# A linear-attention block and a gated feed-forward block on one core: another order of the first loads, of the first products and of the whole plan

## The chip, the cores and the metric

The kernel runs on one core of a Trainium2 chip. The core has five engines that work side by side, each through its own queue in order: TensorE (PE in the profile; its weight loads are the row PEld), VectorE (DVE), ScalarE (ACT), GpSimd (POOL), and SyncE (SP), which in this kernel only starts transfers. ACT starts transfers too, from its own queue. The metric is the device time of one execution in microseconds; lower is better. The kernel before takes 274.34 us (median of three runs, 274.33 to 274.36).

## The reference

One layer over 2048 rows of 640 numbers, in bf16: an attention with a feature map (32 heads of 20), then a feed-forward block with a product as its gate, each behind a layer norm and with a residual.

```python
qkv = layernorm(x) @ wqkv                    # 640 -> 3 * 640, 32 heads of 20
pq, pk = q @ w_phi, k @ w_phi                # per head, 20 x 20
phi_q = concat(softmax(pq), softmax(-pq))    # 40 features per head; phi_k the same from pk
kv  = sum over rows of phi_k^T v ;  z = sum over rows of phi_k
o   = (phi_q @ kv) / (phi_q @ z + 1e-6)
h   = x + o @ wo
out = h + ((n @ w_gate) * (n @ w_up)) @ w_down,   n = layernorm(h);  640 -> 1536 -> 640
```

## The kernel before, in words

The 2048 rows are 16 row tiles of 128. The program is a list of named operations (`G.op`), each with an engine, the buffers it reads and writes, and a key. The string `PLAN` gives each name its key, the engine where there is a choice (`alts`, picked by the second field) and the buffer slots (third field: the eight PSUM banks, `xn`, `ek`, `ph` and the rest). `arrange` sorts by key: so the order on every engine and every transfer queue is written out by hand in `PLAN`, and an instruction that waits holds back everything behind it on its engine. `emit` puts in the semaphore waits that the buffers ask for. The numbers in a name are row tile, part or feed-forward block; the steps that the text speaks of:

- **Loads** (`dma`, L283 to L285; issued from SP or ACT): `x0`, `x1` ... rows of x, one or two tiles each (160 KB a tile); `wk0` to `wk4` and `wv0` to `wv4` the K and V columns of `wqkv` in five row blocks (160 KB each); `w5` the small feature weights; `wqt` the Q columns, turned by a DMA transpose (L309, SP); `wu`, `wg`, `wd`, `wo` the other weights (320 to 480 KB a piece).
- **Warm-up** (`warm`, L366 to L372): ten products of zeros, 512 wide, into PSUM, which need only a cleared buffer.
- **Folding the feature weights into `wk`**: `Ph` (L380) spreads `w5` into block-diagonal pieces; `WT` (L392) turns a row block of `wk` by five 128-wide products with the identity, `WTe` (L251) copies the result out of PSUM; `F1` (L411) multiplies it with the pieces, `Fe1` (L251) copies the folded weights out. `F0`, `Fe0` do this for Q later.
- **First layer norm**: `L1s`, `L1a` statistics (DVE, L428, L431), `L1l`, `L1e` the logarithm and exponential for 1/sqrt (ACT, L436, L439) for the groups of tiles in `LNG`, `L1n` a small product (POOL, L443), `xn` the normalised tile (L451 on ACT, L453 on DVE). Then the tile is turned: for the tiles in `TPE` by five products with the identity (`xt` on PE, L462, and a copy `xte`), for the others by a DMA transpose from SP (`xt`, L471).
- **Projections** (`proj`, L482): `K`, `V`, `Q` of a tile are ten products each of 128 x 320; for tiles 0 and 1 (`TSPLIT`) `K`, `V` (and `Q`) are cut in five pairs, one for each row block of the weights, so that a pair can start when its block is folded.
- **K side**: `Kx` exponentials (ACT, L494), `Ks` sums (DVE, L498), `Kr`, `Ke` their inverse (ACT, L501, L503), `Kn` the scaling (POOL, L518, 1280 wide), `Ve` the copy of V (L251), `KV` (PE, L526) adds the tile's outer products in two PSUM banks. After all 16 tiles `KVe` (DVE, L533) takes them out.
- **Q side**: `Qx` exponentials (ACT, L553, L554), `Qs` sums (DVE, L557), `Qr`, `Qe` (ACT, L560, L567) with a difference `Qb` (POOL, L564) between them, `Qn` the scaling of one half (POOL, L571, 660 wide), `qT` a DMA transpose (SP, L576).
- **Attention out**: `N` (PE, L589), `dd`, `rd`, `o` the division (DVE, L600 to L606), `oT` a DMA transpose (SP), `O` (PE, L616), `h` (DVE, L620), second norm `L2s`, `L2a`, `L2v` (POOL, L630), `L2r`, `hc` the centred tile (L639), `hT` a DMA transpose (SP, L643).
- **Feed-forward** in five blocks of 256 or 512 rows (`FB`): `U` (PE, L658) 24 groups of five products a block, gate and up; `g` (ACT, L663), `u` (DVE, L666); `D` (PE, L677) per row tile, `y` (DVE, L689), `w` the store (SP, L691). The last tile is cut in three column parts (`LASTCUT`).

The stretch in which all Q, K and V products stand runs from about 11 to 76 us; the first `N`, `O` and `U` are mixed in from 76 us on.

Of the kernel before, what the change touches and what calls it, by code (L numbers as in the profile page):

```python
# [48 lines left out]
x0:0.7:1 w5:1.18:1 wk0:1.18 wv0:4.06 wk1:2.14 wv1:2.62 wk2:1.66:1 wv2:3.58:1 wk3:2.62:1 wv3:4.06 wk4:3.1 wv4:4.54:1 x1:0.7 x2:2.14:1 x3:1.66 x4:3.58:1  # L49
x6:3.1 x8:5.02:1 x10:5.02 x12:4.54:1 x14:21.015 wqt0:13.874 wqt1:9.289 wqt2:26.055 wqt3:6.94 wqt4:19.655 wo0:27.415 wo2:34.715 wd0:35.195 wd1:47.175  # L50
wd2:49.392 wd3:37.595 wg0:32.875 wu0:5.5 wg1:37.115 wu1:6.46 wg2:40.335 wu2:25.575 wg3:36.635 wu3:5.98 wg4:35.675 wu4:36.155 id0:0.9 gl0:1.2 eps:0.7
id1:1.45 gla0:2.07 glb0:2.51 gla4:2.29 glb4:4.51 gla1:2.73 glb1:3.17 gla2:3.39 glb2:4.73 gla3:1.85 glb3:2.95 va1:6.664 phz:3.61 ekz:6.364 rqz:6.064
Sz:7.734 mk0:6.164 mk1:7.484 mk2:7.934 zero:0.7 warm0:1.08 warm1:1.51 warm2:1.94 warm3:2.37 warm4:2.8 warm5:3.23 warm6:3.66 warm7:4.09 warm8:4.52::0
warm9:4.74 Ph0:4.95 Ph1:5.609 Ph2:5.743:1 WT0:4.96::1 WTe0:5.509 WT1:6.769::5 WTe1:7.329:1 WT2:5.836::0 WTe2:6.386 WT3:7.725::2 WTe3:8.85 WT4:8.886::0
WTe4:9.922 F1_0:6.342::6 Fe1_0:8.676:1 F1_1:8.162::4 Fe1_1:9.299 F1_2:7.219::0 Fe1_2:8.052:1 F1_3:9.509::6 Fe1_3:10.766 F1_4:10.953::0 Fe1_4:11.538:1
L1s0:3.993 L1a0:5.633 L1s1:4.813 L1a1:6.1 L1s2:7.03 L1a2:9.686 L1s3:6.21 L1a3:10.215 L1s4:11.145 L1a4:12.785 L1s5:11.965 L1a5:13.005 L1s6:13.115
L1a6:14.353 L1s7:10.325 L1a7:12.895 L1s8:20.053 L1a8:21.803 L1s9:20.983 L1a9:23.833 L1s10:14.463 L1a10:20.873 L1s11:15.283 L1a11:19.443 L1s12:28.423
L1a12:34.233 L1s13:25.363 L1a13:30.243 L1s14:26.183 L1a14:34.123 L1s15:31.773 L1a15:34.013 L1l0:6.132 L1e0:7.229 L1l1:7.009 L1e1:7.952 L1l2:10.546
L1e2:11.389 L1n2:11.899 L1n3:11.699 L1l4:14.835 L1e4:15.678 L1n4:16.588 L1n5:16.188 L1n6:16.388 L1n7:15.988 L1l8:24.376 L1e8:24.806 L1n8:28.209
L1n9:28.409 L1n10:25.45 L1n11:25.65 L1l12:34.675 L1e12:35.518 L1n12:35.895 L1n13:36.095 L1n14:38.854 L1n15:36.295 xn0:7.85::0 xt0:8.53::3 xte0:9.268:1  # L60
xn1:8.35::1 xt1:9.165::1 xte1:9.796:1 xn2:12.875:1:3 xt2:17.252::7 xte2:17.978 xn3:12.161:1:2 xt3:13.17::0 xte3:13.935:1 xn4:19.553::2 xt4:21.495
xn5:17.025:1:0 xt5:18.295 xn6:18.943::1 xt6:22.855 xn7:23.333::3 xt7:24.215 xn8:29.243::1 xt8:30.155 xn9:29.743::3 xt9:31.515 xn10:26.408:1:0
xt10:27.895 xn11:27.745:1:2 xt11:33.355 xn12:36.631:1:0 xt12:45.815 xn13:36.758::1 xt13:38.075 xn14:39.692::2 xt14:47.712 xn15:38.118:1:3 xt15:40.815
V0_0:14.536::0 V0_1:14.807 V0_2:15.079 V0_3:15.351 V0_4:15.622 Ve0:20.238::2 K0_0:9.866::2 K0_1:10.138 K0_2:10.681 K0_3:12.083 K0_4:12.898
# [12 lines left out]
KV12:73.164 V13:60.939::4 Ve13:63.15:1:5 K13:50.484::2 Kx13_0:52.165::1 Kx13_1:52.998 Ks13:53.92::0 Kr13:56.436 Ke13:57.479 Kn13:57.839 KV13:73.479
V14:67.73::2 Ve14:69.782:1:7 K14:65.014::4 Kx14_0:66.642::3 Kx14_1:67.529 Ks14:68.362::3 Kr14:70.209 Ke14:70.659 Kn14:71.163 KV14:73.795 V15:70.447::6
Ve15:72.075:1:6 K15:59.58::2 Kx15_0:61.84::2 Kx15_1:62.733 Ks15:63.901::2 Kr15:65.742 Ke15:66.192 Kn15:67.259 KV15:74.11 KVe0:74.956 KVe1:74.696
F0_0:35.421::6 Fe0_0:36.006:1 F0_1:36.682::4 Fe0_1:37.345 F0_2:35.736::2 Fe0_2:37.258:1 F0_3:33.432::2 Fe0_3:34.895 F0_4:38.356::4 Fe0_4:38.941:1  # L80
# [837 lines left out]
```

## Time and profile before

| | |
|---|---|
| median of three runs | 274.34 us |
| the profiled execution: its span, first to last instruction | 272.2 us |
| what lies around the span, to the median | 2.14 us |
| PE busy | 266.0 us (98%), 2103 products |
| DVE, ACT, POOL busy | 171.0, 116.6, 73.9 us |
| TensorE clock granted, all stretches | 1.00 |
| HBM read, written | 11.00 MB, 2.62 MB |

The profile is of one execution; its own time is the span and the 2.14 us around it. A row names the line of the kernel, the engine, the operation and what it writes and reads. A recorded product includes its way through the array, so a 320-wide one is shown as 299 ns although the next starts 136 ns later (30 of them take 4.08 us in the chain of waits): starts tell more than busy time. Recorded spans on DVE and ACT likewise reach about 0.1 us into the next instruction's.

### The profile page before, as it was taken

Reading aid. Unit: us, or ns where it says so; the run is one execution under the profiler, and the core shown is the slowest. Engines: PE = TensorE matmul, PEld = TensorE weight load, DVE = VectorE, ACT = ScalarE, POOL = GpSimd, SP = SyncE. Lnnn points to the kernel's source line nnn. Section 1 sums busy time; section 2 is a strip of 40 time slices with the busy share of each in tenths; the row PEclk is TensorE's granted clock in tenths of the full one; section 3 lists DMA queues with packets and bytes.
Section 4 is the critical chain, followed back from the end, with each engine's and each line's share of the span. In section 5 each row is a group of like instructions: output and inputs, shape, how many; then the busy total and the mean of one; then the engine's idle time right before and its main releaser. Section 6 shows DMA issues by size and latency. Waiting matters only on the chain.

```text
span 272.2 us, 5234 instructions
## 1 busy us (share of the span) xinstructions
PE 266.0 (98%) x2103; PEld 177.2 (65%) x2103; DVE 171.0 (63%) x315; ACT 116.6 (43%) x307; POOL 73.9 (27%) x107
## 2 busy tenths in 40 slices
PE   7899999999989999999999999999999999999996
PEld 2777787777776788775555877766444457544774
DVE  4999978788899999897186147843324022314423
ACT  2999998987766746012213332300332220023000
POOL 7227996899974133200000000000000000000000
DMA  7997999987548998964022001531100001100011
GB/s 201 375 265 162 176 264 313 234 157 108 107 78 160 147 185 110 165 130 98 0 48 48 2 1 43 100 95 43 31 0 2 0 0 51 48 0 0 26 48 55
DMA packets 66600, 27.76 MB, mean 102 GB/s; under 512 B 57744, under 2 KB 65296, under 8 KB 66576
## 3 DMA queue, kind: packets, MB, share of 16 engines
q1 hardware_dynamic: 64752, 25.30, 45.2%
q10 hardware_dynamic: 1824, 2.13, 2.3%
q8 instruction: 16, 0.26, 0.5%
q14 instruction: 8, 0.07, 0.1%
HBM read 11.00 MB, written 2.62 MB: 50 GB/s over the span
## 4 chain that ended last, share of the span: by engine, by line
PE 93%; ACT 3%; DMA 2%; ACTq 1%; issue 0%; DVE 0%; DVEq 0%
PE ps L658 38%; PE ps L482 23%; PE ps L677 19%; PE ps L616 8%; DMA ev<-in_A_wqkv_dram 2%; PE ps L526 2%; ACT ph L553 2%; PE ps L589 1%; PE ps L411 1%; ACTq L285 1%; PE ps L462 0%; ACT ph L554 0%; PE ps L392 0%; ACT L884 0%; DVE Wp L689 0%
## 5 line engine op out<-in xcount | busy, mean ns | idle before, releaser
L658 PE MATMUL ps<-xnT,Wgu 128*128 128x512 bf16 (+1 forms) x600 | 105.2, 336 | 0.0
L658 PEld LDWEIGHTS ps<-xnT,Wgu 128*128 128x128 bf16 x600 | 58.5, 98 | 44.2 <-DVE ev L666 0.4
L663 ACT ACTIVATE gt<-ps 128x512 bf16<-128x512 f32 (+1 forms) x60 | 30.5, 511 | 91.4 <-PE ps L658 74.0
L482 PE MATMUL ps<-Wp,xnT 128*128 128x320 bf16 (+1 forms) x480 | 68.6, 299 | 0.8 <-ACT ph L554 0.8
L666 DVE TENSOR_TENSOR ev<-ps,gt 128x512 bf16<-128x512 f32 (+1 forms) x60 | 32.8, 577 | 47.4 <-PE ps L658 34.0
L482 PEld LDWEIGHTS ps<-Wp,xnT 128*128 128x128 bf16 x480 | 45.6, 97 | 18.4 <-ACT ph L554 0.9
L677 PE MATMUL ps<-Wd,ev 128*128 128x320 bf16 (+2 forms) x396 | 53.7, 295 | 0.0
L677 PEld LDWEIGHTS ps<-Wd,ev 128*128 128x128 bf16 x396 | 38.0, 98 | 14.5
L518 POOL TENSOR_TENSOR ek<-ek,SR 128x1280 bf16<-128x1280 bf16 x16 | 37.6, 2357 | 6.7 <-ACT SR L503 6.6
L689 DVE SCALAR_TENSOR_TENSOR Wp<-ps,rs,x_all 128x640 bf16<-128x640 f32 (+3 forms) x18 | 14.5, 808 | 32.9 <-PE ps L677 32.7
L553 ACT ACTIVATE ph<-ps 128x300 bf16<-128x300 f32 x64 | 23.8, 442 | 7.9 <-PE ps L482 7.4
L630 POOL TENSOR_SCALAR ln<-mv 128x1 f32<-128x1 f32 x16 | 3.3, 210 | 84.6 <-DVE mv L629 73.4
L557 DVE TENSOR_REDUCE S<-ph 128x66 f32<-128x1320 bf16 x16 | 24.2, 1515 | 3.1 <-ACT ph L554 3.1
L498 DVE TENSOR_REDUCE SR<-ek 128x64 f32<-128x1280 bf16 x16 | 23.4, 1472 | 1.3 <-ACT ek L494 1.2
L616 PE MATMUL ps<-Wo,Wp 128*128 128x320 bf16 x160 | 23.9, 299 | 0.3 <-ACT RQ L567 0.3
L494 ACT ACTIVATE ek<-ps 128x640 bf16<-128x640 f32 x32 | 22.3, 714 | 2.7 <-PE ps L482 2.4
L571 POOL TENSOR_TENSOR ph<-ph,RQ 128x660 bf16<-128x660 bf16 x16 | 20.9, 1307 | 6.2 <-ACT RQ L567 6.2
L639 ACT ACTIVATE xn<-x_all,mv 128x640 bf16<-128x640 bf16 x13 | 10.7, 828 | 24.2 <-DVE mv L629 24.2
L616 PEld LDWEIGHTS ps<-Wo,Wp 128*128 128x128 bf16 x160 | 15.2, 98 | 6.6 <-issue 0.6
L620 DVE TENSOR_TENSOR x_all<-ps,x_all 128x640 bf16<-128x640 f32 x16 | 13.0, 813 | 4.5 <-PE ps L616 4.4
L606 DVE TENSOR_TENSOR o<-ps,sm 128x720 bf16<-128x720 f32 x16 | 14.2, 894 | 0.1
L428 DVE BATCH_NORM_STATS2 st<-x_all 128x6 f32<-128x320 bf16 x16 | 7.6, 472 | 3.3 <-DMA x_all<-in_A_x_dram 3.3
(63 smaller groups left out, 171.4 us busy)
## 6 DMA issues: line engine op xcount, KB each, us to landing
out_dram<-Wp SPq DMA_DIRECT2D x15, 160.0 KB, 1.8
Wgu<-in_B_w_up_dram SPq DMA_DIRECT2D x5, 384.0 KB, 9.7
Wgu<-in_B_w_gate_dram SPq DMA_DIRECT2D x5, 384.0 KB, 7.0
Wd<-in_B_w_down_dram SPq DMA_DIRECT2D x4, 480.0 KB, 6.3
x_all<-in_A_x_dram SPq DMA_DIRECT2D x3, 320.0 KB, 6.8
x_all<-in_A_x_dram ACTq DMA_DIRECT2D x3, 320.0 KB, 9.1
Wp<-in_A_wqkv_dram SPq DMA_DIRECT2D x4, 160.0 KB, 7.4
x_all<-in_A_x_dram ACTq DMA_DIRECT2D x3, 160.0 KB, 4.9
```

The costliest lines, as they stand in the source:

```text
L482: ins = e.matmul(pb(b, hb)[:, 0:n1 - n0], lhsT=T["xnT"][:, NC - 1 - c, P * t:P * (t + 1)], rhs=T["Wp"][:, POS[kind], c, n0:n1], start=(c = ...
L494: G.op("act", "%sx%d_%d" % (nm, t, s), lambda e, s=s, b=b, ek=ek: e.activation(out=T["ek"][:, ek.slots[0], 0:2 * D].rearrange("p (b h s f) ...
L498: G.op("dve", "%ss%d" % (nm, t), lambda e, ek=ek, sr=sr: e.tensor_reduce(out=T["SR"][:, sr.slots[0], 0, :], in_=T["ek"][:, ek.slots[0], 0: ...
L518: G.op("pool", "Kn%d" % t, lambda e, ek=ek, sr=sr: e.tensor_tensor(out=T["ek"][:, ek.slots[0], 0:2 * D].rearrange("p (h f) -> p h f", f=DH ...
L553: e.activation(out=o_, in_=i_.rearrange("p (g j f) -> p g j f", j=3, f=DH), func=AF.Exp, scale=1.0 - 2.0 * sg)
L557: G.op("dve", "Qs%d" % t, lambda e, t=t, ph=ph: e.tensor_reduce(out=T["S"][:, t, 0:66].rearrange("p (g k) -> p g k", k=6), in_=pv(ph).rear ...
L571: return e.tensor_tensor(out=v, in0=v, in1=T["RQ"][:, rq.slots[0], 1, 0:33].rearrange("p (g j) -> p g j", j=3).unsqueeze(3).to_broadcast([ ...
L616: ins = e.matmul(pb(b, hb)[:, 0:320], lhsT=T["oT"][:, oT.slots[0], c, :], rhs=T["Wo"][:, c, 320 * hb:320 * (hb + 1)], start=(c == 0), stop ...
L658: ins = e.matmul(pb(b)[:, 0:n], lhsT=T["Wgu"][:, gu, c, P * ft:P * (ft + 1)], rhs=T["xnT"][:, NC - 1 - c, o0:o0 + n], start=(c == 0), stop ...
L663: G.op("act", "g%d_%d" % (bi, ft), lambda e, pg=pg, gt=gt, n=n: e.activation(out=T["gt"][:, gt.slots[0], 0:n], in_=pb(pg)[:, 0:n], func=AF ...
L666: o_ = G.op("dve", "u%d_%d" % (bi, ft), lambda e, pu=pu, gt=gt, hh=hh, ft=ft, n=n: e.tensor_tensor(out=T["hh"][:, hh.slots[0], ft, 0:n], i ...
L677: ins = e.matmul(pb(b, hb)[:, 0:w], lhsT=T["hh"][:, hh.slots[0], ft, P * tt:P * (tt + 1)], rhs=T["Wd"][:, ft, c0 + w * hb:c0 + w * (hb + 1 ...
```

## The change

It changes constants, gives four POOL operations a second engine, and replaces `PLAN`.

- `TPE` is (0, 1) where it was (0, 1, 2, 3): tiles 2 and 3 are turned by a DMA transpose from SP, which takes two times five products off PE, and two copies out of PSUM (`xte2`, `xte3`) off ACT and DVE.
- `NWARM` is 8 where it was 10; behind them come `NFILL` = 5 products of zeros, 256 wide, which stand between the first `WT` and `F1` in the new order.
- `LNG` groups the first layer norm finer: nine groups where there were six.
- `LASTCUT` cuts the last tile at 320 and 576 where it was 320 and 512.
- `L1n`, `Kn`, `Qb`, `Qn` and `L2v` may stand on DVE. In the new `PLAN` DVE has six `L1n`, six `Qb` (tiles 1, 2, 9, 10, 12, 14), four `Qn` (tiles 0, 1, 2, 4) and five `L2v`; no `Kn`. In turn two `Ve` are on DVE where it had six.
- `PLAN` has a new key for every operation. First loads: before, SP issued x1, w5, wk2, wk1, wv1, x6, wv2, wv3, wv4, x10, wu0, wu3, wu1, then three `wqt`; ACT issued x0, wk0, x3, x2, wk3, wk4, x4, wv0, x12, x8. After, ACT issues w5 and wk2 alone; SP issues x0, x1, wk1, wk0, x3, wk4, wk3, wv2, wv1, x4, wv0, x2, x6, wv3, wv4, then wqt1, xt3, x8, xt5, xt2, xt4. The large weights wu0, wu1, wu3 stand far later on SP, wu2 on ACT.
- PE's first products after: warm0 to warm7, WT2, warm8 to warm11, WT1, WT0, warm12, xt0, F1_2, F1_1, WT3, F1_0, WT4, xt1, F1_3, F1_4, then K0, K1, V1, V0 in pairs, V3, K3, V5, K2. Before, F1_4 and xt3 stood between those pairs, and xt2 behind V3.
- ACT after: L1l0, L1e0, WTe2, L1l1, L1e1, WTe0, xte0, Fe1_1, WTe3, Fe1_0, L1l3, L1e3, Fe1_3, xn3, Fe1_4.
- Around the first attention tiles PE has after: KV15, Q7, N0, N1, Q11, N2, Q8, N3, N9, Q14, O0, O1, O2, N4, O3, O9, Q12, N5, Q15, N7, then the first `U`. Before: KV15, Q7, N1, N3, N0, Q11, Q8, N2, Q14, N9, O1, O0, Q12, N5, O3, Q15, N4, N7, O2, O9, then the first `U`. In the new plan Q11 has the two PSUM banks that the KV sums leave; in the old one it had those of Q7.

```diff
-LNG = [[0], [1], [2, 3], [4, 5, 6, 7], [8, 9, 10, 11], [12, 13, 14, 15]]
-TPE = (0, 1, 2, 3)
+LNG = [[0], [1], [2], [3], [4, 5], [6, 7], [8, 9], [10, 11], [12, 13, 14, 15]]
+TPE = (0, 1)
-NWARM = 10
-LASTCUT = [(0, 320), (320, 512), (512, 640)]
+NWARM = 8
+NFILL = 5
+LASTCUT = [(0, 320), (320, 576), (576, 640)]
...
+    for k in range(NWARM, NWARM + NFILL):
+        G.op("pe", "warm%d" % k, lambda e: e.matmul(pb(wm_b)[:, 0:256], lhsT=T["zero"][:, 0:P], rhs=T["zero"][:, 0:256],
+             start=True, stop=True), 0.22, LT, [z_b], [wm_b], -89, before=[G.by["warm%d" % j] for j in range(k)])
...
-                G.op("pool", "L1n%d" % t, lambda e, t=t: e.tensor_scalar(
+                G.op("pool", "L1n%d" % t, lambda e, eng, t=t: e.tensor_scalar(
...
-                    op1=ALU.mult), 0.2, LP, [rs_b[t], mv_b[t]], [nb_b[t]], 10 * t - 25)
+                    op1=ALU.mult), 0.2, LP, [rs_b[t], mv_b[t]], [nb_b[t]], 10 * t - 25, alts=[("dve", 0.07, LD)])
...
-        G.op("pool", "Qb%d" % t, qb, 0.24, LP, [rq], [rq], kk)
+        G.op("pool", "Qb%d" % t, qb, 0.24, LP, [rq], [rq], kk, alts=[("dve", 0.1, LD)])
...
-        G.op("pool", "Qn%d" % t, qn, pool_c(660), LP, [ph, rq], [ph], kk)
+        G.op("pool", "Qn%d" % t, qn, pool_c(660), LP, [ph, rq], [ph], kk, alts=[("dve", dve_c(660), LD)])
...
```

More of the change, by code (lines that the diff above doesn't have):

```diff
@@ L48 @@
 for _t in """
[L49 to L64, printed above, removed]
@@ L77 @@
[L77 to L80, printed above, removed]
@@ new lines @@
+L1s1:4.207 L1a1:5.117 L1l1:6.053 wk1:1.74 L1e1:6.379 warm8:5.266::1 warm9:5.481 wk0:2.22:1 warm10:5.696 warm11:5.91 x3:2.7:1 xn0:5.226::0 gla4:3.14 WT1:6.125::2
+WTe1:6.745 glb4:3.369 WT0:6.543::3 wk4:3.18:1 gla3:3.509 glb3:3.737 Ph2:3.966 wk3:3.66 xn1:7.153::1 warm12:6.96 wv2:4.14:1 WTe0:7.162 Ph0:4.56 wv1:4.62
+L1s3:7.665 xt0:7.175::1 xte0:7.747 x4:5.1 gla2:5.154 glb2:5.383 Ph1:5.612 F1_2:7.454::4 Fe1_2:8.452 F1_1:7.772::6 Fe1_1:8.331 WT3:8.091::0 WTe3:8.915:1
+F1_0:8.508::2 Fe1_0:9.5:1 L1a3:9.192 WT4:8.828::1 WTe4:9.447:1 L1l3:10.084 L1e3:10.41 xt1:9.245::6 xte1:9.855:1 F1_3:9.676::4 F1_4:9.995::0 Fe1_3:10.503
@@ new lines @@
+L1s4:10.263 wv0:5.58:1 K0_0:10.314::2 K1_0:10.585::6 K1_1:10.856 K1_2:11.127 L1s5:11.05 L1n3:10.69 xn3:11.087:1:2 va1:10.914 Fe1_4:11.892:1 L1a4:11.837
+Sz:11.744 L1a5:11.96 L1l4:12.476 L1e4:12.802 x2:6.06 x6:6.54 L1s2:12.069 L1a2:12.979 L1l2:13.212 wv3:7.02 L1s7:13.088 wv4:7.5:1 L1e2:13.538 K0_1:11.398
+wqt1:7.98 xt3:12.03 K1_3:11.669 V1_0:11.94::4 K0_2:12.211 K0_3:12.482 K0_4:12.753 x8:13.34 L1n5:13.082 xn5:13.875::3 Kx0_0:13.631::0 Kx0_1:14.215 L1a7:14.387
+K1_4:13.024 xt5:14.5 Kx1_0:14.799::1 Kx1_1:15.383 V0_0:13.295::0 L1n4:13.306 V1_1:13.566 V1_2:13.837 V1_3:14.108 V1_4:14.379 xn4:15.967:1:0 L1n2:14.496:1
@@ new lines @@
+xn2:14.65::1 xt2:15.81 Ks0:15.162::0 Kr0:16.772 Ke0:17.063 Kn0:17.397 V0_1:14.65 V0_2:14.921 xt4:17.12 V0_3:15.192 V0_4:15.463 V3:15.734::2 Ve3:17.29::0
+L1s6:16.555 L1a6:17.465 Ve1:17.874::1 Ve0:18.458::2 Ks1:17.574::1 Kr1:19.086 L1l6:19.232 L1e6:19.558 Ke1:19.651 L1s9:18.967 L1a9:19.877 K3:17.09::6 L1n7:19.838
+xn7:20.14::2 L1s8:20.652 L1a8:21.562 V5:18.446::2 Ve5:20.002::3 K2:19.802::4 Kx3_0:20.586::2 Kx3_1:21.17 KV0:21.158::0,1 Kn1:20.062 L1l8:21.795 L1e8:22.121
+Kx2_0:22.214::3 K4:21.491::2 Ks3:21.906::2 L1n6:23.299:1 V2:22.847::6 L1n9:22.401 xn9:23.344::3 KV1:24.203 xn6:23.856::1 wqt3:18.43 Kx2_1:22.798 Ks2:24.368::3
```

184 lines of the change are left out of this document (93 added, 91 removed).

## The prediction

> **What bounds the kernel now.** I read the page's busy table first, then the chain of waits, then the timeline of the first 26 us and of the 76 to 96 us stretch, then the busy time by stretches.
>
> ```profile
> PE 266.0 (98%) x2103; PEld 177.2 (65%) x2103; DVE 171.0 (63%) x315; ACT 116.6 (43%) x307; POOL 73.9 (27%) x107
> ```
>
> PE is the bound. The chain says how much of its time is work:
>
> ```profile
> 3.25 6.60 DMA ev<-in_A_wqkv_dram
> 9.89 0.45 PE ps L392 x5
> ...
> 10.94 1.09 PE ps L482 x8
> ...
> 18.61 4.08 PE ps L482 x30
> ...
> 77.64 0.73 ACT ph L553 x2
> ...
> 252.37 17.30 PE ps L677 x132
> ...
> 269.76 0.42 DVE Wp L689
> ```
>
> A 320-wide product costs 0.136 us (4.08/30), so a ten-product K, V or O is 1.36, a Q 1.37, a KV or N 0.33, a turn by five 128-wide products 0.28 and an F1 0.32. Two places are not work. The chain begins with the load wk4, and the first projection starts at 10.78 (timeline); before it PE did seven turns and four F1, 7 x 0.28 + 4 x 0.32 = 3.24, so 7.5 us went to waiting and warm-up. The second: from Q7 (76.01) to the first U (95.74) PE does 6 Q, 8 N and 5 O, 6 x 1.37 + 8 x 0.33 + 5 x 1.36 = 17.7 of 19.7 us: 2.0 lost, the chain passing through ACT's exponentials. Elsewhere PE starts follow each other almost without a gap: about 0.4 us are lost between 11 and 76, none I can find after 96. So 9.9 us can be won at most by order, and the rest only by taking products away.
>
> ```profile
> 6.25 0.45 PE L392 MATMUL ps<-ident,ev 128*128 128x128 bf16 x5 [0.41 <-DMA ev<-in_A_wqkv_dram]
> 6.60 0.49 DVE L428 BATCH_NORM_STATS2 st<-x_all 128x6 f32<-128x320 bf16 x1 [0.41 <-DMA x_all<-in_A_x_dram]
> 7.25 0.69 ACT L251 ACTIVATE scratch<-ps 128x640 bf16<-128x640 bf16 x1
> 8.79 1.90 ACT L251 ACTIVATE Wp<-ps 128x640 bf16<-128x640 f32 x3
> 9.89 0.45 PE L392 MATMUL ps<-ident,ev 128*128 128x128 bf16 x5 [0.17 <-DMA ev<-in_A_wqkv_dram]
> ```
>
> These show arrival order: the fourth and fifth 160 KB load (wk2, x3) release work at 6.25 and 6.60, wk4, the tenth, only at 9.89. They also give the spacing on ACT: three copies of 640 in 1.90, 0.58 from start to start plus 0.7 for the last.
>
> **The change, part by part.** The profiled execution is 272.2 us of span; the median of the runs is 274.34, 2.14 more, and I carry that 2.14 over.
>
> *First loads and the fold.* In the new order wk0 is the fifth 160 KB load (x0, wk2, x1, wk1, wk0) and nothing of wv, x2 or the big weights stands ahead of the wk's. I let it land at 6.5, as the fifth did. Its turn starts 6.55, five starts 0.055 apart and 0.3 to the copy give WTe0 on ACT at 7.1. From there ACT is the chain: WTe0, xte0, Fe1_1, WTe3, then Fe1_0: 4 x 0.58 + 0.70 after 7.1 is 10.1, and the first K starts at 10.2. ACT is free to do this since it issues two loads where it issued ten (the last ended at 6.42, and WTe0 started at 6.46 although WT0 was done at 5.84). The other loads come in time: wk4 and wk3 are seventh and eighth, where the seventh (x2) released DVE at 7.78 and the ninth (wk3) PE at 8.67; the last wv has as many bytes ahead of it as before, where V1's pairs met no DMA wait from 13.3 on, and is asked for at 14. The next edge is Fe1_4: ACT does L1l3, L1e3 (0.4), Fe1_3, xn3 (0.81), Fe1_4 and ends at 12.6; PE asks for it nine pairs (9 x 0.272) after 10.2, at 12.65.
>
> Worth: the first K 0.55 earlier, with F1_4 (0.32) already behind it, and xt2, xt3 (0.56) not on PE at all: 1.4 us. Bounds: if loads land as the first four (by 4.6, then 0.45 each) the chain starts at L1e1, 6.6, and K at 9.7: 1.95. If one queue delivers slower, wk0 as late as the sixth load (wk1, used at 7.58), K starts at 11.25: 0.4. Fifteen loads at 0.4 to 0.6 of SP time each end at 8 to 9, which is before they land, so I stay with 1.4.
>
> *Tiles 2 and 3 by DMA.* xn3 ends at 11.9, SP's transpose takes 1.23 and lands 2.7 us after its start in the median, 9.9 behind six large weights (xt13). V3 asks for it 20 pairs after 10.2, at 15.7; the transpose lands at 14.6 to 15. Before it on SP stands wqt1, and such a transpose held SP 2.6 and 4.3 us at this time: from 8.0 to 10.6 or 12.3, the last a wait of 0.4 that still lands by 15.4. Cost 0, up to 1. xt5, xt2, xt4 follow with 1.3 us each for a tile that costs PE 2.72.
>
> *Warm-up and fills.* 8 x 0.43 end at 4.65, when wk2 is about there; the five fills stand where PE waits for wk1 and wk0. No cost.
>
> *Scaling on VectorE.* Not in the trace: a 660-wide scaling on DVE. Ends: 0.50, like the 640-wide xn (L453), and 1.31, like POOL's own. Nearest is o (L606, 720 wide, 0.894, next start at 0.81): I take 0.85. Four of these, six Qb at 0.1 to 0.24 and the L1n and L2v at 0.1 add 4.5 us to DVE; four `Ve` at 0.73 leave it. In the crowded stretch, from V9 to Q7 in the new order, PE has 17 projections and 7 KV, 25.5 us; DVE has 5 K sums (1.40), 8 Q sums (1.44), 4 Qn, 2 Ve and small ones, 23.6.
>
> ```profile
> 40.00:60.00 20.00, 20.00 (x193) 14.77 (x190) 16.96 (x14) 17.41 (x60) 16.14 (x11) 1.00 1.04 244
> 60.00:80.00 20.00, 19.20 (x210) 14.43 (x208) 17.61 (x21) 15.20 (x60) 18.09 (x18) 1.00 0.55 94
> 80.00:95.00 15.00, 14.66 (x148) 10.57 (x147) 14.79 (x28) 10.35 (x39) 5.19 (x9) 1.00 0.94 161
> ```
>
> (Columns: stretch, length, then busy PE, PEld, DVE, ACT, POOL, the granted clock, DMA share, GB/s.) So DVE keeps 1.9 us to spare: cost 0, but little cover. POOL loses 5 us of work it has room for.
>
> *The passage to attention out.* Q11 no longer waits for Q7's exponentials (the 0.96 us gap at 78.4) since it has the KV banks, and N, Q and O alternate. What remains is DVE: a tile's division is 0.11 + 0.28 + 0.81 = 1.2; three of them and the 0.5 of N come to 4.1 to 4.7 after N0, and PE asks for the third tile's banks (Q14) 5 x 0.33 + 2 x 1.37 = 4.4 after it. I leave 0.4 of the 2.0 lost: 1.6 won. Bounds: 2.0, and 0 if the waits only move. Transposes there land 2.6 (oT, hT) to 3.8 (qT) after issue, and one in the old run took 5.3; that is most of the 0.4.
>
> *Middle and end.* The 0.4 of small gaps stays. The last part is 256 wide, not 192: y at 0.42 gains 64 columns at 1.03 ns (0.88 at 640): 0.07 more. Feed-forward: same products, same copies, no gap before: 0.
>
> Sum: 272.2 - 1.4 - 1.6 + 0.1 = 269.3 of span, 271.4 us.
>
> **The rivals.**
>
> *VectorE and GpSimd block each other.* Place: 51 to 70 us, three Qb and four Qn on DVE while POOL is busy 80 to 90% with 2.36 us Kn and 1.31 us Qn. If a two-input DVE instruction waits for POOL's running one, five separate waits of half a Kn (1.18) are 5.9 us; 1.9 are spare, 4.0 reach PE through Qs, Qr and the Q banks: 275.4, slower. It decides from 4.9 us of waits (1.9 + 3.0); at 0.9 each it is a draw, 274.1. For it and against it:
>
> ```profile
> 4.70 1.07 POOL L380 TENSOR_TENSOR Phi<-w,GL 128x280 bf16<-128x280 bf16 x2 [1.00 <-DMA w<-in_A_w_phi_dram]
> 5.51 0.56 DVE L380 TENSOR_TENSOR Phi<-w,GL 128x280 bf16<-128x280 bf16 x1
> ```
>
> The one such DVE instruction, started while POOL did the same, took 0.56 where 280 columns at 1.03 to 1.13 ns and 0.13 fixed make 0.43: 0.13 too long, while POOL had 0.2 left. But xn on DVE is 0.59 with POOL idle (8.59) and 0.56 inside a Kn (20.12). [...] I give it 0.29: 0.17 for the draw, 0.12 for slower.
>
> *The passage gains nothing.* The exponentials of ACT, the oT transposes or DVE (99% busy from 80 to 95) make other gaps of the same 2.0: 273.0. For it: DVE's share. Against: DVE's rows there hold norm statistics that can wait. 0.10.
>
> *The clock or a load comes late.* The first eight wide products start 0.43 apart, later ones 0.22; the full rate is there at 5.39, after 4.1 us without a pause. New is a break at 4.65. If the rate came a few us later, 3.5 us of turns and F1 would take up to twice as long beside ACT's chain, or V3 waits 1 us for xt3: 272.6. 0.08.
>
> **How the numbers follow.** The forecast, 270.4 to 272.3, has 0.53: its low end is both gains at their bounds (0.5 + 0.4 below 271.4). The rivals hold 0.29, 0.10 and 0.08. Less than 0.2% (0.55 us) either way I call the same: 273.8 to 274.9. Faster is the forecast, the second and third rival, and a sixth of the draws: 0.74; same the rest of the draws, 0.14; slower 0.12. The range runs from 270.4 to 274.6: above lie the slower cases and few draws.
>
> **What would show it.** First K at 10.2 (not 10.8) in the timeline; V3 with no DMA wait; the L571 group on DVE near 0.85 us and POOL's Kn still 2.36 (right), or L571 and L564 on DVE at 1.5 and more with PE waiting for ACT ph between 60 and 76 (first rival); the PE share from KV15 to the first U at 17.7 of about 18.1 us; the last product ending near 266.8. I would be wrong if DVE, with 1.9 us spare in 25, is the bound of the whole projection stretch.

## The result and the profile after

The changed kernel takes 277.28 us (median of four runs, 277.18 to 277.77) beside 274.33 for the kernel before: ratio 1.0118, 95% interval 1.0104 to 1.0133. It is slower by 1.2%, where 271.4 was forecast. The profiled execution has a span of 275.4 us against 272.2, with the clock at 1.00 throughout.

The busy row of the page of after:

```profile
PE 266.6 (97%) x2096; PEld 176.6 (64%) x2096; DVE 180.3 (65%) x335; ACT 114.9 (42%) x311; POOL 67.7 (25%) x87
```

PE is still the bound, and DVE is busy 9.3 us longer than before: 3.9 of it are waits (below), and 3.0 are the `xn` of five more tiles, all done by 50.2 us, which the list of changes leaves out. The chain that ended last in after, in order of time (start, length, what), says where PE was not the last to be waited for:

```profile
10.32 9.52 PE ps L479 x70
...
35.14 6.79 DMA xnT<-xn
...
57.56 0.85 DVE RQ L561
58.41 1.51 DVE ph L568 x2
...
65.58 1.45 DVE RQ L561
...
68.47 2.38 DVE ph L568
70.85 0.75 DVE ev L247
...
90.96 5.24 DMA scratch<-ph
...
115.42 4.81 DMA Wp<-o
...
272.86 0.48 DVE Wp L687
```

The first K starts at 10.16 instead of 10.78 (timelines; the chain counts from the end of the product before, so it has 10.32), as forecast. Then come things that the chain of before did not have: a DMA transpose that took 6.8 us (xt11), a whole stretch of DVE in which `Qb` (L561, RQ) and `Qn` (L568, ph) last 0.85, 1.45 and 2.38 us, and two more transposes of 5.2 and 4.8 us (qT7, oT10).

I measured what PE lost from the starts of its products, less the time per product that the prediction gives:

| PE loses, us | before | after |
|---|---|---|
| until the first K | 7.5 | 6.6 |
| K6, F0_3, K11, K12: tiles and `wqt` that land late | 0.2 | 2.4 |
| V14, V13: PSUM banks that come free late (Qx13 on ACT behind `Qb2`, Ve12 on DVE behind `Qn2`) | 0 | 1.9 |
| from KV15 to the first U | 1.9 | 1.2 |
| O10: oT10 lands late | 0 | 0.9 |
| gaps below 0.15 | 0.4 | 0.7 |
| sum | 10.0 | 13.7 |

The sum is 3.7 more; the turns of tiles 2 and 3 that are no longer on PE take 0.56 off, and 3.1 of the 3.2 us of span are accounted for. The second row, in the timeline of after (start, length, engine, line; in brackets the idle time ahead and what ended it):

```profile
30.23 1.53 PE L479 MATMUL ps<-Wp,xnT 128*128 128x320 bf16 x10 [0.21 <-DMA xnT<-xn]
32.92 0.49 PE L408 MATMUL ps<-Phi,scratch 128*128 128x140 bf16 x6 [1.16 <-DMA scratch<-in_A_wqkv_dram]
```

K6 waits for xt6 and F0_3 for wqt0. xt6 was issued at 24.81 and landed at 30.18, wqt0 at 27.43 and 32.88: 5.4 us each, where a transpose with little ahead of it took 2.6 to 2.7 (xt4, xt9; 3.0 for wqt3). In SP's queue the new plan has x10, wg1, x12, wu4 and x14 in the 5.4 us ahead of xt6 (0.3 to 0.4 MB each), and wu1, wu3, wd2, wd1 right ahead of xt11, which took 6.8.

The third row, in the timeline of after, with a DVE instruction of another kind for comparison:

```profile
46.25 2.35 POOL L515 TENSOR_TENSOR ek<-ek,SR 128x1280 bf16<-128x1280 bf16 x1
47.60 0.60 DVE L450 TENSOR_SCALAR xn<-x_all,mv,rs 128x640 bf16<-128x640 bf16 x1
...
64.62 2.36 POOL L515 TENSOR_TENSOR ek<-ek,SR 128x1280 bf16<-128x1280 bf16 x1
65.50 1.52 DVE L561 TENSOR_TENSOR RQ<-RQ 128x32 f32<-128x32 f32 x1
67.79 2.35 POOL L515 TENSOR_TENSOR ek<-ek,SR 128x1280 bf16<-128x1280 bf16 x1
68.39 2.46 DVE L568 TENSOR_TENSOR ph<-ph,RQ 128x660 bf16<-128x660 bf16 x1
69.11 1.53 PE L479 MATMUL ps<-Wp,xnT 128*128 128x320 bf16 x10 [0.53 <-ACT ph L551]
71.64 0.44 PE L479 MATMUL ps<-Wp,xnT 128*128 128x320 bf16 x2 [1.00 <-DVE ev L247]
```

`Qb2`, 32 numbers wide, takes 1.52 us and ends at 67.03, 0.05 after POOL's Kn13 (66.98). `Qn2` takes 2.46 and ends 0.7 after Kn12 (70.15). Later `Qb`, with POOL idle, take 0.18, and the `Qn` that met nothing 0.83. So four of the ten waited: Qb1 0.2, Qb9 0.75, Qb2 1.35, Qn2 1.6, together 3.9 us. xn12, inside Kn8, did not wait. Nothing in the program makes `Qb2` wait for POOL; its one semaphore wait is for ACT. Behind `Qb2` on ACT's side stands Qe2 and behind that Qx13, for which V14 waits; behind `Qn2` on DVE stands Ve12, for which V13 waits.

The busy time by stretches in after (stretch, length, then PE, PEld, DVE, ACT, POOL):

```profile
40.00:60.00 20.00, 19.62 (x190) 14.25 (x189) 18.04 (x20) 18.32 (x64) 12.64 (x12) 1.00 0.84 158
60.00:80.00 20.00, 18.47 (x185) 13.17 (x184) 19.45 (x16) 15.31 (x55) 17.02 (x14) 1.00 0.91 212
80.00:95.00 15.00, 14.85 (x158) 10.82 (x157) 14.05 (x30) 8.85 (x32) 4.50 (x6) 1.00 0.91 144
```

DVE is at 19.45 of 20 us from 60 to 80, where it had 17.61, and PE falls from 19.20 to 18.47.

### The profile page after: what moved, and what is told of

Read it like the earlier page. It is cut to its first block, busy times and chain, and to the rows that moved or that the text cites. A ratio compares the mean times of both kernels' runs of the same rounds, so it can differ in the third digit from the quotient of the medians.

```text
span 275.4 us, 5224 instructions
## 1 busy us (share of the span) xinstructions
PE 266.6 (97%) x2096; PEld 176.6 (64%) x2096; DVE 180.3 (65%) x335; ACT 114.9 (42%) x311; POOL 67.7 (25%) x87
## 4 chain that ended last, share of the span: by engine, by line
PE 69%; DVE 18%; DMA 6%; ACT 3%; issue 1%; SPq 1%; DVEq 0%
PE ps L656 37%; PE ps L675 18%; PE ps L479 7%; PE ps L613 5%; DVE SR L495 4%; DVE S L554 4%; DMA xnT<-xn 2%; DMA scratch<-ph 2%; DMA Wp<-o 2%; DVE o L603 2%; DVE ph L568 1%; PE ps L364 1%; DVE xn L450 1%; DVE RQ L561 1%; ACT ek L491 1%
## 5 line engine op out<-in xcount | busy, mean ns | idle before, releaser
L656 PE MATMUL ps<-xnT,Wgu 128*128 128x512 bf16 (+1 forms) x600 | 106.7, 336 | 0.6 <-ACT RQ L564 0.6
L661 ACT ACTIVATE gt<-ps 128x512 bf16<-128x512 f32 (+1 forms) x60 | 29.1, 509 | 100.6 <-PE ps L656 83.1
L664 DVE TENSOR_TENSOR ev<-ps,gt 128x512 bf16<-128x512 f32 (+1 forms) x60 | 33.4, 576 | 37.5 <-PE ps L656 27.3
L515 POOL TENSOR_TENSOR ek<-ek,SR 128x1280 bf16<-128x1280 bf16 x16 | 38.2, 2392 | 13.7 <-ACT SR L500 13.6
L491 ACT ACTIVATE ek<-ps 128x640 bf16<-128x640 f32 x32 | 21.2, 736 | 0.8 <-PE ps L479 0.8
L568 POOL TENSOR_TENSOR ph<-ph,RQ 128x660 bf16<-128x660 bf16 x12 | 15.6, 1305 | 17.6 <-ACT RQ L564 17.6
L627 POOL TENSOR_SCALAR ln<-mv 128x1 f32<-128x1 f32 x11 | 2.2, 210 | 47.0 <-DVE rs L630 24.2
L637 ACT ACTIVATE xn<-x_all,mv 128x640 bf16<-128x640 bf16 x11 | 9.0, 827 | 4.1 <-DVE mv L626 4.1
L247 ACT ACTIVATE ev<-ps 128x640 bf16<-128x640 f32 x14 | 9.8, 716 | 1.4 <-PE ps L479 1.1
```

Source lines behind the costliest of these rows:

```text
L491: G.op("act", "%sx%d_%d" % (nm, t, s), lambda e, s=s, b=b, ek=ek: e.activation(out=T["ek"][:, ek.slots[0], 0:2 * D].rearrange("p (b h s f) ...
L515: G.op("pool", "Kn%d" % t, lambda e, eng, ek=ek, sr=sr: e.tensor_tensor(out=T["ek"][:, ek.slots[0], 0:2 * D].rearrange("p (h f) -> p h f", ...
L656: ins = e.matmul(pb(b)[:, 0:n], lhsT=T["Wgu"][:, gu, c, P * ft:P * (ft + 1)], rhs=T["xnT"][:, NC - 1 - c, o0:o0 + n], start=(c == 0), stop ...
L661: G.op("act", "g%d_%d" % (bi, ft), lambda e, pg=pg, gt=gt, n=n: e.activation(out=T["gt"][:, gt.slots[0], 0:n], in_=pb(pg)[:, 0:n], func=AF ...
L664: o_ = G.op("dve", "u%d_%d" % (bi, ft), lambda e, pu=pu, gt=gt, hh=hh, ft=ft, n=n: e.tensor_tensor(out=T["hh"][:, hh.slots[0], ft, 0:n], i ...
```

## The experiments

Two theories, then: A, VectorE's waits behind GpSimd; B, transposes behind bulk loads in SP's queue. Each run is compared with the kernel before on the same chip, by the ratio. The kernel before itself varied between 273.4 and 276.8 on these chips, so ratios and gaps in the trace carry the argument, not single times. In the diffs a line is a `PLAN` entry (name, key, engine, slot); "alt 1" is VectorE.

### Each part undone, and one part alone

`e1`: the ten `Qb` and `Qn` back on GpSimd.

```diff
-Qb1:51.86:1 Qb9:54.788:1 Qn1:54.888:1 Qn0:55.738:1 Qb2:62.244:1 Qn2:64.594:1 Qn4:69.003:1 ...
+Qb1:51.86 Qb9:54.788 Qn1:54.888 Qn0:55.738 Qb2:62.244 Qn2:64.594 Qn4:69.003 ...
```

> The changed kernel with all ten Qb and Qn that it has on VectorE (Qb 1, 2, 9, 10, 12, 14 and Qn 0, 1, 2, 4) back on GpSimd; all else as changed. Theory A (VectorE's two-input instructions wait for GpSimd's running one, and this makes Ve12 and Qx13 late): Qb and Qn no longer wait, and the 1.86 us that TensorE loses before V14 and V13 (67 to 72 us) go: 275.4. Theory B (the loss is transposes behind bulk loads on SP alone): nothing changes before 67 us, and the V14 and V13 waits were an echo of TensorE's earlier lateness: 277.3. Against A's gain stands GpSimd's own load: 20.0 of the 26 us from 50 to 76 are busy, and 4 x 1.31 + 4 x 0.3 = 6.4 come to it, so it has nothing left; if it is late, 276 to 277 with TensorE waiting for KV or qT instead.

Measured: 1.0124 (1.0102 to 1.0145), 277.92 us: no gain. V14 waits 1.95 instead of 0.69: Qb2 now stands behind Kn13 in GpSimd's own queue and is done at 68.2, later than it was on VectorE. V13's 1.17 is gone, KV14 waits 0.66 for Kn14. GpSimd is full, as the last sentence of the expectation has it (20.0 of the 26 us from 50 to 76 busy in after, 6.4 more to come), so the run doesn't tell A from "too much work".

`e2`: only SP's order.

```diff
-wg1:20.22 wu4:23.865 x14:24.345 xt6:24.825 wqt4:26.135 wqt0:27.445 wu1:31.382 wu3:31.862 wd2:32.342 wd1:32.822
-xt11:33.302 wo0:34.612 wo2:46.855 wg0:47.335 xt15:50.435
+wqt4:20.22 xt6:24.82 wqt0:26.14 x14:27.45 xt11:31.7 wg1:32.8 wu4:32.9 wu1:33 wu3:33.1 wo0:38.95
+wd2:39 wd1:39.1 xt15:48.5 wo2:50.5 wg0:50.6
```

> The changed kernel with only SP's queue reordered: wqt4 ahead of xt7, xt6 ahead of wqt0, and the bulk loads wg1, wu4, x14, wu1, wu3, wd1, wd2, wo0, wo2, wg0 behind the transposes xt6, wqt0, xt11, xt10, xt12, xt15 that they stood ahead of. Theory B: the waits of TensorE for xt6 (0.37), wqt0 (1.34), xt11 (0.54) and xt12 (0.14) go, 2.4 us: 274.9. Theory A alone (VectorE is the bound of the stretch from 42 to 76, so an earlier TensorE only waits longer there): the 2.4 comes back before V14 and V13: 277.

Measured: 1.0032 (1.0013 to 1.0052), 275.56 us. PE no longer waits for xt6, wqt0 or xt11; F0_3 now, in the timeline of this run, has no wait noted:

```profile
30.91 0.48 PE L408 MATMUL ps<-Phi,scratch 128*128 128x140 bf16 x6
```

The waits before V14 and V13 are 0.69 and 1.17 as before: they are no echo of the loads, and an earlier PE doesn't pay there. xt6 lands 4.1 us after its issue, wqt0 4.5 and xt11 2.6. So B is a cause of its own, worth 0.9% (1.0118 to 1.0032), 2.4 us; in the trace the 2.4 of gaps are gone and 0.9 come back from the passage on (0.5 of it before O3, for oT3). No run separates whether the transposes wait in SP's queue or for the DMA engines (their share from 28 to 44 us is 1.11 in after, 0.81 in e2).

`e3`: both edits.

> Both edits together (scaling back on GpSimd, bulk loads behind the transposes). If the two causes add, 277.3 - 1.9 - 2.4 = 273.0. If they are one cause (VectorE as the bound), as the better of the two alone, 274.9 to 275.4. If GpSimd is now full, 274 to 275 with TensorE waiting for GpSimd's Kn or for qT.

Measured: 1.0067 (1.0045 to 1.0089). Worse than e2 alone: V14 waits 1.95 and KV14 0.66, as in e1.

`e4`: the kernel before, with eight `Qb` on VectorE and nothing else.

```diff
-Qb0:53.179 Qb1:55.778 Qb2:61.743 Qb3:48.32 Qb4:70.923 Qb5:67.019 Qb9:60.198 Qb13:73.522
+Qb0:53.179:1 Qb1:55.778:1 Qb2:61.743:1 Qb3:48.32:1 Qb4:70.923:1 Qb5:67.019:1 Qb9:60.198:1 Qb13:73.522:1
```

> The kernel before with one thing alone: eight Qb (tiles 0 to 5, 9, 13; 32 numbers wide) on VectorE instead of GpSimd, all else as before. Their work is 8 x 0.18 = 1.4 us, and VectorE has 26 - 23.2 = 2.8 us idle from 50 to 76. If they cost only their work: 274.3 to 274.6. If each waits for the GpSimd instruction that is running (busy 24.4 of these 26 us, Kn 2.36 and Qn 1.31 long, so about 1 us a time), 8 us of waits come to VectorE, 5 more than it has: 277 to 279, with TensorE waiting for ACT's ph or VectorE's ev between 60 and 78.

Measured: 1.0153 (1.0125 to 1.0180), 278.99 us. The timeline of this run, two of the eight:

```profile
55.03 2.36 POOL L518 TENSOR_TENSOR ek<-ek,SR 128x1280 bf16<-128x1280 bf16 x1 [0.29 <-ACT SR L503]
55.38 2.06 DVE L564 TENSOR_TENSOR RQ<-RQ 128x32 f32<-128x32 f32 x1
...
70.50 2.36 POOL L518 TENSOR_TENSOR ek<-ek,SR 128x1280 bf16<-128x1280 bf16 x1
71.24 1.67 DVE L564 TENSOR_TENSOR RQ<-RQ 128x32 f32<-128x32 f32 x1
```

Seven of the eight end 0.05 us after the GpSimd instruction that was running; the eighth met none and took 0.18. Together they took 6.3 us for 1.4 of work. The loss is 4.2 us, of which 0.9 in the profile is xt4 and xt7 landing late. That these seven waited on VectorE until GpSimd's instruction had ended is shown, and that it costs time.

### Can an order live with the waits?

`e5` is e2 with the two operations moved that the waits held up, `e7` the same without e2's loads.

```diff
-Qe2:63.409 Qn2:64.594:1
+Qe2:65 Qn2:65.5:1
```

> The kernel of the reordered loads (275.56) with two operations moved, scaling still on VectorE: on ACT Qe2, which waits for the blocked Qb2, stands behind Qx13 instead of ahead of it; on VectorE Ve12 stands ahead of the blocked Qn2 instead of behind it. Theory A1 (the VectorE waits cost only through what is queued behind them): Qx13 starts at Q13's end, 63.0 instead of 64.9, and Ve12 1.6 us earlier, so the 0.69 and 1.17 that TensorE loses before V14 and V13 go, though VectorE waits as long as before (1.53 and 2.46): 275.56 - 1.86 = 273.7. Theory A2 (VectorE has no room, busy without a gap from 52 to 72, so whatever is moved, its work ends at the same time): a gap of 1 us or more comes back later, before KV14, Q7 or N0: 275.

> The changed kernel with Qe2 and Ve12 moved alone, loads as changed. If the loads and the VectorE waits are two separate causes: 277.3 - 1.9 = 275.4. If the second is an echo of the first (TensorE late, so the order no longer fits): no gain, 277.

Measured: e5 1.0027 (1.0011 to 1.0043), e7 1.0127 (1.0097 to 1.0157). V14 and V13 no longer wait in either, but 1.14 comes back a little later: Q6 waits 0.67 for Ve14, V15 0.29 for Ve13, KV15 0.18 for Ve15, all behind DVE's Qs13 and Ks14. A2, VectorE without room, was nearer than A1. In e7's trace xt6 also landed late enough to cost 2.5, and behind this wait the granted clock was 0.50 from 34 to 37 us, which cost another 1.5; so e7's time doesn't tell what the two moves are worth alone, only its gaps do (1.86 gone, 1.14 back).

`e6` and `e12` add moves in the passage to e5 (wd0 behind the last transposes that U0 waits for, O10 later; e6 also oT3 earlier):

```diff
-wd0:71.471 oT3:83.167::3 O10:113.723::0
+wd0:98 oT3:81.6::3 O10:118.342::0
```

`e9` moves the four that waited to GpSimd, each into a place between two long instructions, with the loads of e2; `e10` adds the moves of e12 to it.

```diff
-Qb1:51.86:1 Qb9:54.788:1 Qb2:62.244:1 Kn13:60.737 Qn2:64.594:1 Qe2:63.409 Ve13:69.853:1:2
+Qb1:51.86 Qb9:54.788 Qb2:61.05 Kn13:61.1 Qn2:65.5 Qe2:65 Ve13:68.9:1:2
```

> As the kernel with Qe2 and Ve12 moved, and three moves more: O10 behind D1_0 and N11 on TensorE (it waited 1.03 for oT10, which lands 2 us late), the load wd0 from ahead of qT5 to behind qT6 on SP, and oT3 ahead of qT13 on SP (TensorE waited 0.54 for it). If these waits are lateness of one transfer each and nothing waits behind them: 273.7 - 1.0 - 0.5 - 0.2 = 272.0, which is faster than the kernel before (274.3). If the time goes to the next thing that is late (h1, Qx12_1 by qT7, the D's): 273 to 273.7.

> The kernel of the reordered loads, with those four scalings that waited on VectorE (Qb1 0.2, Qb9 0.75, Qb2 1.35, Qn2 1.6 us of waiting) back on GpSimd, each where GpSimd is between two long instructions (Qb2 ahead of Kn13, Qn2 right behind Kn12); Qn0, Qn1, Qn4 and the late Qb stay on VectorE. Qe2 stands behind Qx13 on ACT, and Ve13 ahead of Qn4 on VectorE. VectorE gets 4.4 us of its packed stretch from 52 to 72 back. If the waits for GpSimd were what used up VectorE's room: the 1.14 us that TensorE loses before Q6, V15 and KV15 with the waits still there, and the 1.86 before V14 and V13, go; Kn15 and Kn14 are 0.7 later on GpSimd, KV14 loses 0.2: 275.3 - 0.9 = 274.4, ratio 0.999 to 1.000 to the kernel before. If VectorE's work without the waits is already too much: Q6, V15 or KV15 still wait 0.5 and more, 275.3 and ratio 1.003.

> The same, with wd0 from ahead of qT5 to behind qT6 on SP and O10 behind D1_0 and N11 on TensorE, but oT3 left where it was. The waits before O0 (0.38) and O10 (0.93, of which D1_0 takes 0.59 while it waits for o15) shrink: 0.7 less than the kernel without these two, 273.7, ratio 0.997. If an instruction packet then meets a transpose with no slack (as oT9 met one in the run with oT3 moved, 2.08 us): 274.4 to 275.5.

> The reordered loads, Qe2 and Ve12 moved, and wd0 behind qT6 and O10 behind D1_0 and N11, oT3 where it was. From the run with Qe2 and Ve12 moved (ratio 1.0027) 0.4 before O0 and 0.3 before O10 are taken: 274.6, ratio 1.000, if no instruction packet meets a transpose without slack; 275.5 and 1.003 if one does.

Measured: e6 1.0033 (1.0010 to 1.0055), e9 1.0047 (1.0026 to 1.0069), e10 1.0026 (1.0005 to 1.0047), e12 0.9985 (0.9964 to 1.0006). In e9 the waits went to the instructions that had been free of them: Qn1 took 1.99 (it now met Kn10), Qn4 2.72 (Kn15), and Ve10 came late for K15 (0.99). In e6 the 0.53 before O3 went and O9 waited 2.08 for oT9.

`e15` and `e18` go on from e12 and mend the order around the last tiles.

```diff
-Ve14:67.884::3 Ks14:67.61::2 Ve13:69.853:1:2 Qs13:66.175 Qr13:67.738::0 Qn4:69.003:1 qT4:69.981::5
+Ve14:67.5::3 Ks14:66.7::2 Ve13:67.6:1:2 Qs13:67.7 Qr13:73.3::0 Qn4:72 qT4:73::5
```

(e18; e15 has `Qr13:69.5::0` and Ve15 ahead of Qx6 on ACT.)

> The version with Qe2, Ve12, wd0 and O10 moved (ratio 0.9985), and the order around the last tiles mended: Ve14 ahead of Qe4 and Qr13 on ACT, Ks14 and Ve13 ahead of Qs13 on VectorE, Ve15 ahead of Qx6 on ACT, Qn4 on GpSimd behind Kn14. The 0.67, 0.28 and 0.18 that TensorE loses before Q6, V15 and KV15 go: 1.1 us, ratio 0.9945, faster than the kernel before. If VectorE or GpSimd has no room (Qb2 and Qn2 still wait 1.3 and 1 us): the time comes back before KV14, KV15 or N0, ratio 0.998.

> The version with Ve14, Ks14, Ve13 and Qn4 moved, where N0 waited 2.12 for KVe, mended: on ACT Qr13, which held Qx10 for 1.6 while it waited for Qs13, stands behind Ve15, and Qx6 is ahead of Ve15 as before; so Qs10, Qs6 and KVe come 1.8 to 2.1 earlier on VectorE. If nothing else waits: 2.0 under that version, ratio 0.997 to 0.998, and N0 at 76.5 instead of 78.4. If the passage is bound by something else (qT5 by N0, o2, oT3): half of it, ratio 1.001 to 1.002.

Measured: e15 1.0057 (1.0035 to 1.0079), e18 0.9981 (0.9960 to 1.0001), 274.15 us. e15 lost 2.12 before N0, because Qr13 held Qx10 on ACT; without that (e18) PE loses 0.5 from K12 to N0, the largest wait 0.18 for KV15. So an order by hand can live with Qb2's and Qn2's waits, but it takes a move for every instruction behind them, and it ends level with the kernel before, not clearly under it.

### The same work without the wait

Four runs leave the scaling of the ten tiles' parts out: e11, e13, e14 and e17 put a product by a constant or by row numbers in its place, on VectorE and in the same place in the order, so that the form differs and the length little (`Qn` alone takes 0.38, 0.50, 0.50 and 0.60, where it had 0.83; `Qb` 0.18, 0.29, 0.29 and 0.30, where it had 0.18). They show what the wait costs and are no kernels to use. e13 is on the order of the changed kernel, the other three on e2's. In e11, flat on both sides:

```diff
+return e.tensor_scalar(out=T["RQ"][:, rq.slots[0], 1, 0:32], in0=T["RQ"][:, rq.slots[0], 0, 0:32], scalar1=1.0,
+                       scalar2=None, op0=ALU.mult)
...
+return e.tensor_scalar(out=T["ph"][:, ph.slots[0], 0:900], in0=T["ph"][:, ph.slots[0], 0:900], scalar1=1.0,
+                       scalar2=None, op0=ALU.mult)
```

e13 and e14 have xn's two row numbers (mv, rs) in place of the 1.0.

> The kernel of the reordered loads, with Qb (1, 2, 9, 10, 12, 14) and Qn (0, 1, 2, 4) still on VectorE in the same places, but as instructions with one SBUF input: Qb a product of 32 numbers by 1.0, Qn a product of 900 columns of ph by 1.0. So these tiles' scaling is left out; the length of the work is about kept (xn, one input and 640 wide, took 0.59 to 0.61, so 900 wide is near 0.83). In after's trace one-input instructions inside a running Kn were not longer (xn7, xn11, xn12, xn13 0.60 to 0.61), those with two SBUF inputs ended when GpSimd's instruction ended. If the waits for GpSimd are what costs and the place and work of the scaling cost nothing: Qb2 0.2 instead of 1.53, Qn2 0.83 instead of 2.46, the 0.69 and 1.17 before V14 and V13 go and nothing comes back in the stretch: 275.6 - 1.9 = 273.7, ratio 0.996. If VectorE's work is too much without any wait: V14 and V13 or Q6 and V15 still wait 0.5 to 1, 275, ratio 1.001 to 1.003.

> The changed kernel, loads as changed, with Qb (1, 2, 9, 10, 12, 14) and Qn (0, 1, 2, 4) on VectorE in the same places but in the form of xn: one SBUF input, minus one number and times one number of each row (mv, rs), 32 and 900 wide. These tiles' scaling is left out. xn in this form was not longer inside a running Kn (0.60 to 0.61); the form with a constant in the instruction did wait (Qn2 2.03, Qb2 1.08 in the run with one input). If the waits alone cost TensorE the 1.86 before V14 and V13: none of the ten is longer than 0.9, these two gaps go and do not come back: 1.9 under the changed kernel in the same comparison. If VectorE's work is too much without waits: at most 0.5 under it.

> The same with the bulk loads behind the transposes. If waits and loads are the two causes and add up: 277.3 - 1.9 - 1.9 = 273.5, ratio 0.996 to 0.997, which is what the change would be worth with both mended. If a third cause holds the stretch from 52 to 76: 274.5 to 275.5.

> The changed kernel again, unedited, so that the others of this call are compared with it on one chip: 1.011 to 1.013 of the kernel before, with xt6 or wqt0 late by 1 to 2.5 us.

> The kernel of the reordered loads, with Qb (1, 2, 9, 10, 12, 14) and Qn (0, 1, 2, 4) on VectorE in the same places, now with xn's layout too: output written as 5 blocks in reverse order from a flat input of 640 (Qn), 11 blocks of 3 from 33 (Qb). These tiles' scaling is left out. The flat 900-wide and 32-wide forms took 0.50 and 0.29 when alone, and still waited beside GpSimd (Qb9 0.94, Qb2 1.09, Qn2 2.03); xn's layout took 0.60 for 640 and did not wait. If the waits are the cause: no Qn above 0.65, no Qb above 0.35, TensorE loses nothing before V14 and V13 (0.15 and 0.66 with the flat form, 0.69 and 1.17 with the kernel's own), 273.5, ratio 0.995 to 0.997. If VectorE's work is the cause: V14, V13 or Q6 and V15 still wait 0.5 and more in all, ratio 1.000 to 1.002 as with the flat form.

Measured: e11 0.9999 (0.9976 to 1.0022); e16, the changed kernel again, 1.0130 (1.0106 to 1.0154); beside it e13 1.0117 (1.0084 to 1.0150) and e14 1.0017 (0.9998 to 1.0036); e17 0.9955 (0.9933 to 0.9976), 273.49 us.

e13 is 0.13% under e16, 0.4 us, and e14 0.15% under e2, within both intervals. My expectation for e11, e13 and e14, that one input does not wait, was wrong: Qb2 took 1.08 to 1.09 and Qn2 2.03 in all three. So these three test neither of the two cases that their expectations tell apart: 3.1 to 3.5 of the 3.9 us of waits were still there, and so were 0.8 of the 1.9 us before V14 and V13. What xn has beside its one input is its layout: the output is written as five blocks in reverse. In e17 the ten have that too:

```diff
+return e.tensor_scalar(out=T["ph"][:, ph.slots[0], 704:1344].rearrange("p (c n) -> p c n", c=5)[:, ::-1, :],
+                       in0=T["ph"][:, ph.slots[0], 0:640].rearrange("p (c n) -> p c n", c=5),
+                       scalar1=T["mv"][:, t, 0:1], scalar2=T["rs"][:, t:t + 1], op0=ALU.subtract, op1=ALU.mult)
```

The groups of `Qn` and `Qb` on DVE (busy and mean ns) in e14:

```profile
L571 DVE TENSOR_SCALAR ph<-ph,mv,rs 128x900 bf16<-128x900 bf16 x4 | 3.5, 883 | 0.0
L562 DVE TENSOR_SCALAR RQ<-RQ,mv,rs 128x32 f32<-128x32 f32 x6 | 3.3, 548 | 0.3 <-ACT RQ L557 0.3
```

and in e17:

```profile
L572 DVE TENSOR_SCALAR ph<-ph,mv,rs 128x640 bf16<-128x640 bf16 x4 | 2.3, 602 | 0.0
L562 DVE TENSOR_SCALAR RQ<-RQ,mv,rs 128x33 f32<-128x33 f32 x6 | 1.8, 304 | 0.3 <-ACT RQ L557 0.3
```

Alone, the flat forms of e14 took 0.50 and 0.29, so their means carry 3.1 us of waits; those of e17 take 0.60 and 0.30 each time, inside Kn too, and wait for nothing. The work is no less in e17, only the wait is gone, and the time goes from 1.0017 to 0.9955: 1.7 us for 3.1 us of waits (from e11, with 3.5 us of waits and 0.9999, it is 1.2). From e2 (3.9 us of waits, and Qn 0.2 longer) it is 2.1. In e17 PE runs through the stretch:

```profile
60.00:80.00 20.00, 20.00 (x226) 15.13 (x224) 16.99 (x23) 15.86 (x60) 13.77 (x14) 1.00 0.97 213
```

So the waits, not the work, used up VectorE's room: from the first K to the passage at 80 PE waits for nothing on VectorE, only 0.43 for xt6 and 0.14 for xt8. The two-input `Qb` and `Qn` waited for a running GpSimd instruction in four of ten cases in after (3.9 us) and in seven of eight in e4. Of the one-input forms the flat ones, 900 and 32 wide, waited too (Qn2 2.03, Qb2 1.09 in e14), and those in reversed blocks, 640 in five and 33 in eleven, did not (0.60 and 0.30 in e17). Which part of the form decides it was not shown: no run here has the blocks without the reversal.

### The late transposes

In after's trace 16 packets of 16 KB run on the page's queue of instructions:

```profile
q8 instruction: 16, 0.26, 0.4%
```

`e8` shifts them with 40 more small products in the head (45 fills of 16 columns for 5 of 256).

> The changed kernel with the five fills of 256 columns replaced by 45 of 16 columns, which stand where TensorE waits for wk1. The trace of after has 16 packets of 16 KB on the queue of instructions, about one for 263 TensorE instructions (2 x 2103 / 16), each 0.9 to 1.5 us long; the transposes that took 4.8 to 5.4 us instead of 2.7 and 3.7 (qT7, qT6, qT11, oT10) were under way at 94.33, 106.82 and 117.55, when such a packet went. 80 instructions more bring the packets 0.3 of their spacing forward: 117.6 to about 114, 106.8 to 103, 94.3 to 90.5. If the packets cause the late landings: oT10 lands 2.7 after its issue and TensorE's 0.91 us wait before O10 goes, qT7 lands 3.7 after its issue, and other transposes, those under way at 90.5, 103 and 114, take 1.5 to 2.5 longer: 276.3 if these have slack, 277.3 if not. If the packets have nothing to do with it: the same four transposes late, O10 waiting 0.9, 277.3 to 277.6.

Measured: 1.0205 (1.0180 to 1.0230). The packets went at 91.5, 104.2 and 118.1 instead of 94.3, 106.8 and 117.5. The late transposes changed with them: oT3 (4.7 after issue), qT10 (5.3), hT2 (4.2) and oT5 (4.4) were late, qT7 4.3 instead of 5.2, oT10 4.3 instead of 4.8. O3 now waits for oT3, in the timeline of e8:

```profile
93.60 0.58 PE L613 MATMUL ps<-Wo,Wp 128*128 128x320 bf16 x3 [1.66 <-DMA Wp<-o]
```

and in that of after O10 for oT10:

```profile
120.28 0.99 PE L613 MATMUL ps<-Wo,Wp 128*128 128x320 bf16 x6 [0.74 <-DMA Wp<-o]
```

My forecast of where they would go (90.5, 103, 114) held for the first two within 1.2 us and missed the third, which came 4 later, and oT10 did not become punctual. But over all 20 traces, from 76 us on, 110 of the 177 transposes with such a packet under way between issue and landing landed more than 1 us late (later than 2.7 us after issue, 3.7 for a `qT`), and none of the 666 others. That the two go together is shown; by what means is open.

## Why the prediction was wrong, step by step

- **First loads and the fold: right.** First K at 10.16 (10.2 forecast; 9.85 to 10.53 in the other traces of this head), F1_4 already done, xt2 and xt3 off PE: 0.62 + 0.32 + 0.56 = 1.5 where 1.4 was forecast. wk0 landed at 6.43 (6.5).
- **Tiles 2 and 3 by DMA, warm-up and fills: right.** xt3 landed at 15.42, V3 started at 15.59 without a wait; no cost in either.
- **"The 0.4 of small gaps stays": the step that failed most.** It stood for everything from 16 to 76 us that waits for a load, and was never worked out: I costed the first fifteen loads and wqt1 to xt4, but not wg1, x10, x12, wu4, x14, wu1, wu3, wd2 and wd1 in their new places in SP's queue, which xt6, wqt4, wqt0 and xt11 are behind. The row that prices this was in the prediction (xt13, 9.9 us behind six large weights), but was used for tiles 2 and 3 alone. The term measured 2.2 us more than before; e2 gives about as much back (0.9%, 2.4 us).
- **"DVE keeps 1.9 us to spare: cost 0, but little cover": failed.** The first rival's mechanism is what happened, at a lower price: four waits of 3.9 us in all (it had five of 1.18), 1.9 us on PE by the gaps and 1.2 to 2.1 by e17. By the rival's own sum (1.9 of 3.9 hidden) 2.0 remain. Added alone to the forecast they give 273.4, still faster than before. I gave it 0.29 because xn inside a Kn did not wait, and xn, with one input and its layout, did not wait in the runs either (mean 0.59 us in after, e4, e9, e11, e14 and e17, as in before): the row was the wrong witness for an instruction with two inputs.
- **The passage, 1.6 won: mis-sized.** PE lost 1.2 from N9 to the first U, not 0.4: 0.7 won. Q11 is free of Q7's exponentials as said; U0 waits 0.7 behind Qx12 on ACT, which needs the buffer that qT7 frees, 5.2 us after its issue.
- **"Feed-forward: no gap before: 0": failed by 0.9.** O10 has no slack for oT10, which landed 4.8 after issue.

1.9 + 2.2 + 0.9 + 0.9 is 5.9, the distance from 271.4 to 277.3. That it comes out so evenly is in part luck: the span is 6.1 above the forecast's 269.3 (the gaps below 0.15 cost 0.3 more than before, the head gained 0.1 more than forecast), and the time lies 1.7 to 1.8 us above the span in this run and in those of the experiments, where the text before the prediction has 2.14 around it and the prediction carried that over. With loads and waits both mended (e17, which leaves the ten tiles' scaling out) the time is 273.5 on a chip where the kernel before took 274.9: what the passage and O10 keep is the rest.
